# Attention and expert layer on one core: first weight loaded by head halves and split in place, state products in three passes, state reads in column tiles

## The chip, the cores and the metric

The kernel runs on one core of a Trainium2 chip. The metric is the device time of one execution in microseconds (us). The kernel before took 666.48, 667.12 and 668.52 us in three runs; the median is 667.12 us. Engines are called by the profile's short names: PE is the matrix engine (PEld its weight loads), DVE the vector engine, ACT the scalar engine, POOL the general engine, SP the engine whose queue issues most transfers.

## The reference

Eight batches, eight heads, 512 tokens and 32 state rows of 64 numbers per head. Tokens attend to the state rows and the state rows attend to the tokens; the results stand side by side as 544 rows of 512 numbers, and each row goes through a layer norm and a two-layer product with 2048 hidden units.

```python
def _attn_ref(x, state):            # x: 8,8,512,64   state: 8,8,32,64
    scores = scale * x @ state^T;  a = softmax(scores);   xread = a @ state
    scores2 = scale * state @ x^T; a2 = softmax(scores2); sread = a2 @ x
    return concatenate([xread, sread], axis=2)

def _moe_ref(x, g_ln, w_ch1, w_ch2):   # x: 8,544,512  w_ch1: 512,2048  w_ch2: 2048,512
    xn = (x - mean) / sqrt(var + 1e-06) * g_ln
    return x + maximum(xn @ w_ch1, 0.0) @ w_ch2
```

The two weights arrive as 64-bit floats, 8.4 MB each.

## The kernel before, in words

Every number that goes into a product is scaled and split into a high and a low 16-bit part; a product then takes three of the four pairs of parts (`TERMS`). Heads are numbered 4g + j: g is one of two halves of the heads, j one of four heads within a half. The weights are worked on in four units u of 512 hidden columns.

*The head of the program.* `weights1(u)` loads unit u of the first weight in two transfers of 1 MB (L587, 128 partitions by 8 KB, tiles `raw` and `sums`), puts the two 32-bit words of each number together (`words`, on ACT and DVE, tile `w_t`), takes the mean over the rows out (`means` on PE, L601, then four updates of `w_t` on DVE), finds the largest column sum on PE (L610) for the scale, and splits the unit into halves in `raw` or `sums`. Four transfers of 256 KB from 64 partitions to 64 partitions then bring the halves into `w1c[u]`, so that a high part on one set of 64 partitions stands opposite a low part on the other.
`attention(0)` runs among this: batch 0's tokens are split and transposed by two DMA transposes (`xT`, two halves of the tokens), the state by one (`sT`). The score products (L405) make four groups of eight products, two per half of the tokens; softmax follows on DVE and ACT (`mp`, `mB`, `eB`, `ts`, `ea`). `read_state` (L481) multiplies the tokens by the state's softmax, 32 products of 128 by 128 by 64, and `fold_halves` (L494) adds the halves with four 32-bit products by a folded identity.
`state_products(b)` (L667) multiplies the state of a batch by `w1c`: for each unit and each g eight products of 128 rows, 32 columns (a column tile of the array) and 512 values, two passes of four column tiles. ACT and DVE split the result into `matrix[b][u]`. Because a token's attention is a mixture of 32 state rows, the first layer of the tokens is a product of `matrix` with the softmax (`first_products` L703 for batch 0, `first` L801 for the others).
`weights2` loads and splits the second weight; `second_products_by_unit` (L717) makes batch 0's second layer.

*The body.* From batch 1 on `products(b)` makes the first layer in blocks (L801, tile `half`) and the second by Strassen's scheme with seven sums (L857, tile `acc`), while `attention(b+1)` and `state_products(b+1)` for the next batch run among it.

*The end.* The 256 state rows (`state_rows`) go through the first layer by `w1c` itself (`first_of_state`, L810) and a copy of its high parts (`high_halves`), then through the second.

*What sets the order.* All work stands in lists of steps (`streams`). `PLAN` is a written-out string of entries "stream:steps"; `issue` runs it through, and each engine's instructions, the transfers on SP's queue too, stand in exactly that order. `WARM` products of a constant tile `ones` into a spare tile (L188, tile `half`) are among the steps; nothing reads them. Most instructions carry the line of the helper `do` (L188), so they are told apart by their tiles.

*On-chip sums.* PE writes to three pools: `acc` (four tiles), `banks` (one tile of two banks, used by scores, state reads and token mixtures) and `half` (two tiles).

The steps that the change touches: L299 (`gx`), L477 to L496 (`read_state`, `fold_halves`), L586 to L623 (`weights1`), L662 to L677 (`state_products`), L806 (`first_of_state`), L893 (`high_halves`), `state_rows`, `PLAN` and `WARM`.

## Time and profile before

| | |
|---|---|
| three runs | 666.48, 667.12, 668.52 us, median 667.12 |
| span of the profiled execution | 665.1 us (first to last instruction, 14886 instructions); the page gives no other time for it, so the median lies 2.0 us above the span |
| granted clock, mean | 0.996 |
| PE busy | 643.9 us (97%) |
| DVE, ACT, POOL busy | 499.5 (75%), 388.8 (58%), 217.9 us (33%) |
| DMA | 69.64 MB, 105 GB/s on average |

The page cuts the span into 40 slices of 16.6 us; a digit is the busy share of a slice in tenths. The groups' rows give the shapes, the count, the busy time, the mean time of one instruction and the idle time before them. "L857 PE MATMUL acc<-w2h,xs" is a product of line 857 that writes tile `acc` from tiles `w2h` and `xs`. Products overlap in the pipe, so a group of n takes less than n times its mean.

### The profile page before, as it was taken

To read this page: it belongs to the slowest core of one execution; us is meant where nothing else is said; L and a number is where in the kernel's file an instruction comes from. 1 tells how busy PE (TensorE), PEld (TensorE's weight loads), DVE (VectorE), ACT (ScalarE), POOL (GpSimd) and SP (SyncE) were. 2 spreads that over 40 slices of the span, in tenths; PEclk is the share of its full clock that TensorE was granted. 3 is DMA by queue.
4 is the path that set the end of the run, shared out by engine and by line. 5 is a ranking of instruction groups with operands and counts; after the bars stand their busy time and mean duration, and the time that the engine had idled before them with its cause. 6 is when DMAs were issued, how large, how long until landed. Compare 5 with 4: busy or idle time off the path is not lost.

```text
span 665.1 us, 14886 instructions
## 1 busy us (share of the span) xinstructions
PE 643.9 (97%) x6051; PEld 499.6 (75%) x6051; DVE 499.5 (75%) x1002; ACT 388.8 (58%) x699; POOL 217.9 (33%) x189
## 2 busy tenths in 40 slices
PE   7997999999999999999999999999999999999996
PEld 2343655549887887788888888888778887888885
DVE  5998976687788677967887689777976897465533
ACT  5498889667546474547465656465546564344331
POOL 0000443321344315323452226333433343234222
PEclk8999999999999999999999999999999999999999
DMA  8999846825131434340416152405142411245211
GB/s 323 309 276 209 257 130 132 138 57 135 43 67 43 130 105 78 96 100 2 92 33 163 67 88 68 100 2 121 38 125 46 77 33 42 82 116 98 78 57 32
DMA packets 98564, 69.64 MB, mean 105 GB/s; under 512 B 72704, under 2 KB 90624, under 8 KB 98048
## 3 DMA queue, kind: packets, MB, share of 16 engines
q1 hardware_dynamic: 96384, 64.77, 38.4%
q0 software_dynamic: 864, 3.15, 2.5%
q8 instruction: 47, 0.77, 0.5%
q10 hardware_dynamic: 1248, 0.79, 0.4%
q14 instruction: 21, 0.17, 0.1%
HBM read 28.05 MB, written 9.44 MB: 56 GB/s over the span
## 4 chain that ended last, share of the span: by engine, by line
PE 86%; DVE 8%; DMA 3%; ACT 1%; issue 1%; SPq 0%; DVEq 0%
PE acc L857 41%; PE half L801 22%; PE acc L717 6%; PE half L667 5%; PE half L810 3%; DVE w_t L188 2%; PE acc L703 2%; PE acc L749 2%; PE banks L481 1%; PE banks L405 1%; PE banks L517 1%; DMA w1c<-raw 1%; DMA raw<-in_moe_w_ch_dram 1%; PE banks L494 1%; DMA x_f<-in_x_dram 1%
## 5 line engine op out<-in xcount | busy, mean ns | idle before, releaser
L857 PEld LDWEIGHTS <-xs 128*128 128x128 f16 x2520 | 242.4, 98 | 43.6 <-issue 15.3
L188 POOL TENSOR_TENSOR xs<-rs,xs 128x512 f16<-128x512 f32 x120 | 142.5, 1200 | 272.6 <-ACT xs L188 207.1
L857 PE MATMUL acc<-w2h,xs 128*128 128x256 f16 x1440 | 183.0, 273 | 0.0
L801 PE MATMUL half<-ea,matrix 128*128 128x256 f16 x1344 | 159.4, 273 | 0.0
L801 PEld LDWEIGHTS <-matrix 128*128 128x128 f16 x1344 | 130.7, 98 | 16.7 <-issue 0.8
L857 PE MATMUL acc<-sums,xs 128*128 128x256 f16 x1080 | 141.9, 273 | 0.0
L188 DVE SCALAR_TENSOR_TENSOR rs<-half,rs 128x256 f32<-128x256 f32 x224 | 89.4, 419 | 27.6 <-ACT rs L188 13.3
L188 ACT ACTIVATE xs<-rs 128x512 f16<-128x512 f32 x128 | 77.1, 618 | 40.5 <-DVE rs L188 33.8
L188 ACT ACTIVATE xs<-half 128x256 f16<-128x256 f32 (+1 forms) x112 | 53.7, 487 | 73.2 <-PE half L801 51.3
L188 DVE SCALAR_TENSOR_TENSOR xs<-half,xs 128x256 f16<-128x256 f32 (+1 forms) x112 | 61.2, 550 | 28.1 <-ACT xs L188 24.5
L188 ACT ACTIVATE matrix<-half,hs 128x512 f16<-128x512 f32 x56 | 38.1, 687 | 35.2 <-PE half L667 34.9
L188 DVE SCALAR_TENSOR_TENSOR matrix<-half,hs,matrix 128x512 f16<-128x512 f32 x56 | 41.2, 742 | 16.0 <-ACT matrix L188 15.3
L188 ACT ACTIVATE rs<-half 128x256 f32<-128x256 f32 x56 | 21.4, 382 | 42.4 <-PE half L801 40.0
L717 PE MATMUL acc<-w2h,hid 128*128 128x512 f16 x192 | 43.1, 379 | 0.0
L188 DVE TENSOR_TENSOR strip<-acc,strip 128x256 f32<-128x256 f32 (+1 forms) x60 | 33.2, 554 | 10.5 <-PE acc L857 7.5
L667 PE MATMUL half<-w1c,sT 128*32 128x512 f16 x448 | 33.5, 384 | 1.9 <-DVE rs L188 1.0
L717 PEld LDWEIGHTS <-hid 128*128 128x128 f16 x192 | 18.5, 98 | 20.9 <-issue 0.4
L188 POOL TENSOR_TENSOR ts<-ts,mA 128x1024 f32<-128x1024 f32 (+1 forms) x8 | 14.4, 1806 | 59.3 <-DVE mA L188 52.9
L188 PE MATMUL half<-ones 128*128 128x512 bf16 x103 | 28.0, 416 | 1.1 <-DVE ones L309 1.1
L188 DVE SCALAR_TENSOR_TENSOR x<-x_f,x_s,x 128x512 f16<-128x512 f32 x32 | 24.8, 799 | 5.3 <-ACT x L188 5.3
L188 POOL TENSOR_TENSOR hid<-strip,hid 128x512 f16<-128x512 f32 x16 | 19.5, 1232 | 26.9 <-ACT hid L188 26.8
L188 DVE BATCH_NORM_STATS2 s<-xr 128x6 f32<-128x512 f32 x32 | 21.6, 684 | 8.7 <-ACT xr L188 8.6
(154 smaller groups left out, 791.5 us busy)
## 6 DMA issues: line engine op xcount, KB each, us to landing
raw<-in_moe_w_ch_dram SPq DMA_DIRECT2D x9, 1024.0 KB, 8.6
out_dram<-xr SPq DMA_DIRECT2D x16, 512.0 KB, 3.7
x_f<-in_x_dram SPq DMA_DIRECT2D x15, 512.0 KB, 5.0
sums<-in_moe_w_ch_dram SPq DMA_DIRECT2D x7, 1024.0 KB, 8.2
ek<-ea SPq DMA_DIRECT2D x56, 64.0 KB, 2.0
ek<-ek SPq DMA_DIRECT2D x7, 512.0 KB, 4.3
xr<-part POOLq DMA_DIRECT2D x6, 512.0 KB, 5.0
w1c<-raw SPq DMA_DIRECT2D x8, 256.0 KB, 6.8
```

Source lines behind the costliest of these rows:

```text
L188: return lambda: f(*map(now, args), **{k: now(v) for k, v in kw.items()})
L405: nc.tensor.matmul(o[32 * j:32 * j + 32], lhsT=sT[:, g, a, 32 * j:32 * j + 32], rhs=xT[:, s, 4 * g + j].rearrange("p c t -> p (c t)"), sta ...
L481: nc.tensor.matmul(ps_z[:, h // 4, :, h % 4], lhsT=xv[:, c // hc, h, c % hc], rhs=ebT[:, :, h // 4, c, 32 * (h % 4):32 * (h % 4) + 32], st ...
L494: nc.tensor.matmul(pr[:, g], lhsT=z4[:, g, i], rhs=fold, start=i == 0, stop=i == 1, skip_group_check=True)
L517: nc.tensor.matmul(px[:, c, D * h:D * h + D], lhsT=ek[:, h // 4, h % 4, (2 * t + c) * P:(2 * t + c + 1) * P], rhs=sk[:, h], start=True, st ...
L667: nc.tensor.matmul(ps[32 * j:32 * j + 32], lhsT=sT[:, g, a, 32 * j:32 * j + 32], rhs=w[:, 2 * g + j // 2, j % 2], start=a == 0, stop=a == ...
L703: nc.tensor.matmul(o[:, 256 * f:256 * f + 256], lhsT=m[:, g, i, P * (q + f):P * (q + f) + P], rhs=ea[:, s, k, g], start=f == 0 and g == 0 ...
L717: nc.tensor.matmul(po, lhsT=hid[:, i, q, c * P:(c + 1) * P], rhs=w[:, j, q], start=first and q == 0 and n == 0, stop=last and q == 3 and n ...
L749: nc.tensor.matmul(o, lhsT=signs[:, k // 2], rhs=v[k], start=start and k == 0, stop=k == 3, skip_group_check=True)
L801: nc.tensor.matmul(ps[:, 256 * q:256 * q + 256], lhsT=m[:, h, i, P * (2 * k + q):P * (2 * k + q) + P], rhs=ea[:, 0, j, h, 256 * g:256 * g ...
L810: nc.tensor.matmul(ps[:, 256 * q:256 * q + 256].rearrange("p (t n) -> p t n", t=2), lhsT=w[:, k // 2, k % 2, fs] if k < H else wn[:, k - H ...
L857: nc.tensor.matmul(po[o], lhsT=y[:, n, i, o] if o < 2 else x[:, o - 2, n, i], rhs=v[j], start=u == 0 and n == 0 and k == 0 and o in (2, 1, ...
```

## The change

- `weights1` loads by head halves: each 1 MB transfer becomes two of 512 KB, one to partitions 0 to 63 (g = 0), one to partitions 64 to 127 (g = 1). Partition 64g + d then holds row d of the four heads of half g. `gx` is loaded likewise in two.
- The split writes straight into `w1c[u]` (high and low parts one behind the other); the 16 transfers from `raw` and `sums` to `w1c` are gone. So is `high_halves` with its 8 transfers.
- `state_products` makes, for a unit, 24 products of 64 rows, 32 columns and 512 values: three passes (`TERMS`) over four column tiles and two row halves g. From batch 1 on the two g write the two banks of one `banks` tile, and ACT and DVE split both at once (1024 values); before, each g wrote a `half` tile of its own.
- `read_state` makes 64 products: for each j, c and part i one for each g, written to partitions 64g to 64g + 63; the high token part meets both parts of the softmax (64 values), the low part only the high one (32 values). A DVE reduction adds the parts, and one 32-bit transpose by the identity takes the place of the four fold products.
- The state rows are arranged to match: eight blocks of 128 in place of twelve, and the same 12 products for each result.
- `PLAN` is new; `WARM` goes from 103 to 73.

Three places where the order moves, on the engines that wait there. First SP, from the start of the program. Before:

```order
L188 DMA x_f<-in_x_dram 128x4x256
L188 DMA s_j<-in_state_dram 128x2x64
L587 DMA sums<-in_moe_w_ch_dram 128x2x1024 x2
L587 DMA raw<-in_moe_w_ch_dram 128x2x1024 x3
L188 DMA_TRANSPOSE xT<-x_108 128x16x128
L188 DMA_TRANSPOSE sT_224<-sh 128x4x128
L188 DMA_TRANSPOSE xT<-x_108 128x16x128
L587 DMA raw<-in_moe_w_ch_dram 128x2x1024 x2
```

Now:

```order
L187 DMA x_f<-in_x_dram 128x4x256
L187 DMA s_j<-in_state_dram 128x2x64
L585 DMA raw<-in_moe_w_ch_dram 64x2x1024 x2
L585 DMA sums<-in_moe_w_ch_dram 64x2x1024 x2
L585 DMA raw<-in_moe_w_ch_dram 64x2x1024 x6
L585 DMA sums<-in_moe_w_ch_dram 64x2x1024 x2
L585 DMA raw<-in_moe_w_ch_dram 64x2x1024 x2
L585 DMA sums<-in_moe_w_ch_dram 64x2x1024 x2
L187 DMA_TRANSPOSE xT<-x_109 128x16x128
L187 DMA_TRANSPOSE sT_168<-sh 128x4x128
L187 DMA_TRANSPOSE xT<-x_109 128x16x128
```

Before, five of the eight megabytes of the first weight stood ahead of the transposes; now all 16 half transfers do.

Second PE, where the first score products (L405) stand among the means of the weights (L601, now L598); what an instruction waits for stands in brackets. Before, at the second unit's means:

```order
L601 MATMUL acc<-w_t,gm 128x512 [waits DVE_49]
L601 MATMUL acc<-w_t,gm 128x512 x3
L405 LDWEIGHTS sT_224 [waits DMAHW2_49]
L405 MATMUL banks<-xT,sT_224 32x256 [waits DMAHW1_49]
L405 LDWEIGHTS sT_224
```

Now, at the end of the first eight score products:

```order
L405 MATMUL banks<-xT,sT_168 32x256
L598 MATMUL acc<-w_t,gm 128x512 [waits DVE_49]
L598 MATMUL acc<-w_t,gm 128x512 x3
L405 LDWEIGHTS sT_168
L405 MATMUL banks<-xT,sT_168 32x256 [waits DMAHW7_49]
```

Two units' means stand ahead of the score products in both; the third unit's stood behind all 32 of them, with 20 warm products and a column sum between, and now stand right behind the first eight, which wait for the transposes.

Third DVE, around the first reading of the scores (`mp`, the maximum of the state's scores). Before:

```order
L188 STREAM_TRANSPOSE ts<-banks 128x512
L188 SCALAR_TENSOR_TENSOR w_t<-w_t,gx,acc 128x512 x3
L188 TENSOR_REDUCE mA<-ts 128x16
L188 TENSOR_REDUCE of_weights<-acc 128x1
L188 TENSOR_TENSOR ts<-ts,mA 128x512
L188 SCALAR_TENSOR_TENSOR w_t<-w_t,gx,acc 128x512
L188 TENSOR_REDUCE mp<-banks 128x4
L188 TENSOR_REDUCE dA<-ts 128x16
```

Now:

```order
L187 SCALAR_TENSOR_TENSOR w_t<-sums 128x1024
L187 SCALAR_TENSOR_TENSOR w_t<-w_t,gx,acc 128x512 x4
L187 TENSOR_SCALAR sums<-sums 128x1024
L187 TENSOR_SCALAR raw<-raw 128x1024
L187 SCALAR_TENSOR_TENSOR w_t<-w_t,gx,acc 128x512 x3
L187 TENSOR_REDUCE mp<-banks 128x4
L187 TENSOR_TENSOR mB<-mp 128x2
L187 TENSOR_SCALAR mB<-mB,es 128x2
L187 STREAM_TRANSPOSE ts<-banks 128x512
L187 SCALAR_TENSOR_TENSOR w_t<-raw 128x1024
```

The reading of the scores has moved: the words of three units and eleven of their twelve updates now stand ahead of it, and the words of the last unit behind it. From it to the end of the first split into `w1c` it is 32 rows of DVE now, and 32 rows from it to the end of the first split before.

The diff without `PLAN`:

```diff
-WARM = 103
+WARM = 73
...
-    nc.scalar.dma_start(out=gx, in_=g_ln.rearrange("(k p) -> p k", p=P))
+    for g in range(G):
+        nc.scalar.dma_start(out=gx[64 * g:64 * g + 64], in_=g_ln.rearrange("(g j d) -> g d j", g=G, j=4)[g])
...
-        ps_z = pz[:, 0].rearrange("p (g i j n) -> p g i j n", g=G, i=2, j=4)
+        ps_z = pz[:, 0, 0:256].rearrange("p (j i n) -> p j i n", j=4, i=2)
 
         def read_state(ps_z, x16, ebT):
-            xv = x16.rearrange("p (s h c) i d -> p s h c (i d)", s=parts, c=hc)
-            for h in range(H):
+            xv = x16.rearrange("p (s h c) i d -> p s h c i d", s=parts, c=hc)
+            for j in range(4):
                 for c in range(C):
-                    nc.tensor.matmul(ps_z[:, h // 4, :, h % 4], lhsT=xv[:, c // hc, h, c % hc],
-                                     rhs=ebT[:, :, h // 4, c, 32 * (h % 4):32 * (h % 4) + 32],
-                                     start=c == 0, stop=c == C - 1, skip_group_check=True)
+                    for i in range(2):
+                        for g in range(G):
+                            nc.tensor.matmul(ps_z[64 * g:64 * g + 64, j, 0:2 - i], lhsT=xv[:, c // hc, 4 * g + j, c % hc, i],
+                                             rhs=ebT[:, 0:2 - i, g, c, 32 * j:32 * j + 32],
+                                             start=c == 0 and i == 0, stop=c == C - 1, skip_group_check=True)
...
-        yield do(nc.scalar.activation, z, pz[:, 0], AF.Copy)
-        def fold_halves(pr, z4):
-            for g in range(G):
-                for i in range(2):
-                    nc.tensor.matmul(pr[:, g], lhsT=z4[:, g, i], rhs=fold, start=i == 0, stop=i == 1,
-                                     skip_group_check=True)
-        yield do(fold_halves, pr, z4)
+        yield do(nc.vector.tensor_reduce, z.rearrange("p (j n) -> p j n", j=4), ps_z.rearrange("p j i n -> p j n i"), AX.X,
+                 ALU.add)
+        yield do(nc.tensor.transpose, pz[:, 1, 0:P], z, idf)
...
-            nc.sync.dma_start(out=raw.rearrange("p (k f) -> p k f", k=2),
-                              in_=w1[256 * fh:256 * fh + 256, 1024 * u:1024 * u + 1024].rearrange("(k p) f -> p k f",
-                                                                                                  p=P))
+            rows_of = w1[:, 1024 * u:1024 * u + 1024].rearrange("(g j d) f -> g d j f", g=G, j=4)
+            for g in range(G):
+                nc.sync.dma_start(out=raw.rearrange("p (j f) -> p j f", j=2)[64 * g:64 * g + 64],
+                                  in_=rows_of[g, :, 2 * fh:2 * fh + 2])
...
-        hl = raws[1].bitcast(F16).rearrange("p (i e) -> p i e", i=2)
-        yield from split(hl[:, 0], hl[:, 1], t, scale)
-        hl = hl.rearrange("p i (k f) -> p i k f", k=4)
-        w = narrow(u, "w1c").bitcast(F16).rearrange("p (k s f) -> p k s f", k=4, s=2)
-        w1c[u] = w
-        for i in range(2):
-            for s in range(2):
-                to = 64 * (i ^ s)
-                yield do(nc.sync.dma_start, out=w[to:to + 64, :, s], in_=hl[64 * s:64 * s + 64, i])
+        w = narrow(u, "w1c").bitcast(F16).rearrange("p (i e) -> p i e", i=2)
+        yield from split(w[:, 0], w[:, 1], t, scale)
+        w1c[u] = w.rearrange("p i (j f) -> p i j f", j=4)
...
-        def multiply(ps, g, sT, w):
-            for a in range(2):
+        def multiply(ps, sT, w):
+            for n, (i, k) in enumerate(TERMS):
                 for j in range(4):
-                    nc.tensor.matmul(ps[32 * j:32 * j + 32], lhsT=sT[:, g, a, 32 * j:32 * j + 32],
-                                     rhs=w[:, 2 * g + j // 2, j % 2], start=a == 0, stop=a == 1, skip_group_check=True)
+                    for g in range(G):
+                        r = slice(64 * g, 64 * g + 64)
+                        nc.tensor.matmul(ps[g][32 * j:32 * j + 32], lhsT=sT[r, g, i, 32 * j:32 * j + 32], rhs=w[r, k, j],
+                                         start=n == 0, stop=n == 2, skip_group_check=True)
...
-                ps = accumulator() if b == 0 else half()
...
+                ps = banks()
+                scale = hs[:, u:u + 1]
+                yield do(lambda p, *a: multiply([p[:, g] for g in range(G)], *a), ps, sT, w1c[u])
+                yield do(nc.scalar.activation, m[:, :, 0], ps, AF.Copy, scale=scale)
+                yield do(nc.vector.scalar_tensor_tensor, m[:, :, 1], ps, scale, m[:, :, 0], ALU.mult, ALU.subtract)
...
-    def high_halves(u):
-        high[u] = quad("high").bitcast(F16).rearrange("p (k f) -> p k f", k=4)
-        for s in range(2):
-            half = slice(64 * s, 64 * s + 64)
-            yield do(nc.sync.dma_start, out=high[u][half], in_=w1c[u][half, :, s])
```

More of the change, by code (lines that the diff above doesn't have):

```diff
@@ L804, in first, with first_of_state @@
                                                  skip_group_check=True)
[L806 removed]
+                def first_of_state(ps, k, w, xsT):
                     for q in range(2):
[L808 to L812 removed]
+                        fs = slice(P * (2 * k + q), P * (2 * k + q) + P)
+                        for n, (i, x) in enumerate(TERMS):
+                            for j in range(4):
+                                nc.tensor.matmul(ps[:, 256 * q:256 * q + 256].rearrange("p (t n) -> p t n", t=2),
+                                                 lhsT=w[:, i, j, fs], rhs=xsT[:, :, x, j],
+                                                 start=q == 0 and n == 0 and j == 0, stop=n == 2 and j == 3,
+                                                 skip_group_check=True)
                 def strassen_hidden(b=b, g=g, u=u, halves_of=halves_of, x=x, y=y, rs=rs, s=s):
@@ L820, in block @@
                         else:
[L821 removed]
+                            yield do(first_of_state, ps, k, w1c[u], state_rows_T[0])
                             r = rs[:, 512 * k:512 * k + 512]
@@ L939, in moe_attention @@
         streams += these
-    streams += [list(state_rows()), *(list(high_halves(u)) for u in range(U))]
+    streams.append(list(state_rows()))
     streams += [list(s) for s in products(B)]
```

43 lines of the change are left out of this document (19 added, 24 removed), and 242 rows, old and new, of the table PLAN.

## The prediction

> **What bounds the kernel now.** I read the page first, then the busy times by stretch.
>
> ```profile
> span 665.1 us, 14886 instructions
> PE 643.9 (97%) x6051; PEld 499.6 (75%) x6051; DVE 499.5 (75%) x1002; ACT 388.8 (58%) x699; POOL 217.9 (33%) x189
> ...
> PE 86%; DVE 8%; DMA 3%; ACT 1%; issue 1%; SPq 0%; DVEq 0%
> ```
>
> ```profile
> core 0: us, PE busy (x) PEld busy (x) DVE busy (x) ACT busy (x) POOL busy (x), PEclk, DMA share, GB/s
> 0.00:57.90 57.90, 46.37 (x258) 20.79 (x259) 50.20 (x87) 38.73 (x48) 1.75 (x7) 0.97 1.01 289
> 57.90:76.60 18.70, 16.70 (x178) 10.17 (x177) 16.01 (x33) 16.18 (x27) 5.98 (x5) 1.00 0.84 211
> 76.60:138.00 61.40, 61.34 (x429) 35.02 (x429) 45.67 (x88) 50.76 (x79) 23.58 (x22) 1.00 0.66 148
> 138.00:659.40 521.40, 519.43 (x5187) 433.58 (x5186) 385.54 (x794) 283.17 (x546) 186.59 (x156) 1.00 0.31 75
> ```
>
> There are two programs in one. From 76.6 us on PE is busy without a gap worth naming (2 us in 583), so there every microsecond of PE work taken away is a microsecond gained, and nothing else counts. Up to 76.6 us PE is filled up with warm products; the DMA share is about 1, DVE is busy for 66 of 76.6 us, and what counts is when the first state products can start. The chain of waits shows how that came about:
>
> ```profile
> 46.36 1.12 DVE w_t L188
> 47.48 2.27 DVE raw L188
> 49.77 1.37 SPq L188
> 51.19 6.68 DMA w1c<-raw
> 57.92 6.29 DMA raw<-in_moe_w_ch_dram
> ```
>
> DVE ends the first unit's split at 49.7, the transfers into `w1c` take until 57.9, and there PE's first state product starts. So the time is the start of the state products plus PE's work behind it. The change cuts the second and moves the first.
>
> **PE's work behind the head.** The price of a state product group, from PE's timeline:
>
> ```profile
> 299.54 0.38 PE L857 MATMUL acc<-w2h,xs 128*128 128x256 f16 x2
> 299.85 0.62 PE L667 MATMUL half<-w1c,sT 128*32 128x512 f16 x8
> 300.40 0.28 PE L857 MATMUL acc<-sums,xs 128*128 128x256 f16 x1
> ...
> 79.37 1.05 PE L667 MATMUL acc<-w1c,sT 128*32 128x512 f16 x16
> 80.35 1.05 PE L703 MATMUL acc<-ea,matrix 128*128 128x256 f16 x8
> ```
>
> Two passes hold PE from 299.85 to 300.40, 0.55 us; four from 79.37 to 80.35, 0.98. A pass of four column tiles is (0.98 - 0.55) / 2 = 0.215 us. The two plain products before start at 299.54 and 0.11 later, and the next would have started at 299.76, so entering costs 0.09 and leaving 0.12: 0.21 for the change of tiling. A unit's two groups cost 2 x 0.64 = 1.28 apart and 1.07 together; most stand apart. After: one group of three passes, 3 x 0.215 + 0.21 = 0.86, if the two row halves run at once. Saved 0.42 apart, 0.21 together; I take 0.36, and for the 28 units of batches 1 to 7 -10 us. That is 6 to 12 if they do run at once. If they run one after the other it is six passes, 1.50 us, and a loss of 28 x 0.22 to 0.43 = 6 to 12. No row of the trace has two row groups in flight; four column tiles of one pass are, so I take that they do.
>
> ```profile
> 8.15 0.27 PE L188 MATMUL banks<-idf,x_am 128*2 128x128 f32 x1 [3.05 <-DVE x_am L188]
> 8.26 0.50 PE L188 MATMUL half<-ones 128*128 128x512 bf16 x1
> ...
> L494 PE MATMUL banks<-fold,z 128*128 128x64 f32 x64 | 8.2, 272 | 0.5 <-ACT z L188 0.5
> L481 PE MATMUL banks<-ebT,x 128*128 128x64 f16 x256 | 8.8, 193 | 0.0
> ...
> 156.60 1.10 PE L481 MATMUL banks<-ebT,x 128*128 128x64 f16 x32
> 157.53 1.47 PE L801 MATMUL half<-ea,matrix 128*128 128x256 f16 x12
> 158.84 1.00 PE L494 MATMUL banks<-fold,z 128*128 128x64 f32 x8
> 159.68 0.38 PE L749 MATMUL acc<-w2h,signs 128*128 128x256 f16 x2
> ```
>
> The fold costs 159.68 - 158.84 = 0.84 a batch. One transpose of 128 columns lies between 0.11 (the transpose of the two columns of `x_am` starts at 8.15, the product behind it at 8.26) and half the fold, 0.42; I take 0.25: -0.6 x 7 = -4. The state read costs 0.93 for 32 products, 29 ns each. After it is 64 of half the width. If the two column tiles run at once, 16 x (64 + 32) values at 29 ns for 64 are 0.70, with the change of tiling 0.91; if each product keeps its 29 ns it is 2.07. I take 1.25, near the lower end, as column tiles overlap fully in the row above: +0.3 x 7 = +2, between 0 and +8. Against me speaks the Trainium skill, "TensorEngine Tiling (Array Packing)", Gotcha 2: column tiling excludes the fast weight load. By it the 64-column loads would set the pace and the state read would be nearer +8; no run here shows a 64-column load.
>
> Together -12, between -18 and -2. The state rows keep their 12 products a result. DVE gets a reduction in place of ACT's copy of `z`, and the double-width split of `matrix` holds the single `banks` tile longer, but only beside other users of it; with DVE busy 386 of 521 us there I price that at nothing, and at up to +6 where PE meets a `banks` tile still being read.
>
> **The head.** What goes: 4.2 MB of transfers into `w1c`, 7 us of them on the chain. What comes: all of the first weight in transfers to 64 partitions, ahead of the transposes. The rate of the two kinds stands in two windows, 8 to 18 us (loads to 128 partitions) and 51 to 57 us (64 to 64 partitions, alternating halves):
>
> ```profile
> DMA packets 1080, 4.16 MB, mean 416 GB/s; under 512 B 64, under 2 KB 64, under 8 KB 1080
> q1 hardware_dynamic: 1080, 4.16, 102.8%
> ...
> DMA packets 1300, 1.25 MB, mean 209 GB/s; under 512 B 78, under 2 KB 1300, under 8 KB 1300
> q1 hardware_dynamic: 1300, 1.25, 113.4%
> ```
>
> Both keep all 16 engines busy; with 64 partitions they move half as much. I take 209 GB/s for the new loads and keep 416 as the other bound, since the slow rows are copies from one on-chip tile to another and not loads. The Trainium skill, "SBUF — State Buffer", Door 1, says why it would hold for loads too: 64 partitions reach 8 of 16 ports, 196 GB/s measured, and two transfers to both halves gain only 6%. By its 196 the weight would land 3 us later than by the row; the trace agrees with the rule.
>
> ```profile
> 0.74 5.50 DMA x_f<-in_x_dram
> ...
> 15.00 5.06 SPq L188 DMA_TRANSPOSE xT<-x  x1
> 20.18 1.20 SPq L188 DMA_TRANSPOSE sT<-sh  x1
> ...
> 24.45 0.62 PE L405 MATMUL banks<-xT,sT 128*32 128x256 f16 x16
> ...
> 30.16 1.22 DVE L188 TENSOR_REDUCE mp<-banks 128x4 f32<-128x1024 f32 x1
> ...
> 47.40 4.61 DVE L188 SCALAR_TENSOR_TENSOR raw<-w_t,of_weights,raw 128x2048 f16<-128x2048 f32 x2
> ```
>
> The first tokens land at 6.2. Then 8.39 MB at 209 GB/s take 40 us: 46.3. The transposes queue behind: before, the first could be issued at 15.0 and still landed only when the loads ahead had drained (its products start at 24.45). I give it 2 us: 48.3. Then PE's order holds: eight score products 0.5, the third unit's means, 16 and 8 more score products and a column sum:
>
> ```profile
> 16.16 3.70 PE L601 MATMUL acc<-w_t,gm 128*128 128x512 f32 x8 [0.48 <-DVE w_t L188]
> ...
> 26.07 1.02 PE L610 MATMUL acc<-sums,ones 128*128 128x512 bf16 x4 [0.24 <-ACT sums L188]
> ```
>
> 0.5 + 3.5 + 1.0 + 0.9 + 0.5 = 6.4, so `mp` starts at about 54.7. DVE is queued up behind it. From `mp` to the end of the first split it took 47.40 + 2.3 - 30.16 = 19.5 us before for 32 rows; the new 32 rows are of the same kinds, so the first split ends at 74 to 75, and the first state products start there without a transfer, against 57.9: +17. PE stands idle from the second unit's means until the transposes, and cold products cost double:
>
> ```profile
> 1.09 4.01 PE L188 MATMUL half<-ones 128*128 128x512 bf16 x9 [1.09 <-DVE ones L309]
> ...
> 27.79 2.55 PE L188 MATMUL half<-ones 128*128 128x512 bf16 x11
> ```
>
> 0.45 us each at the start, 0.23 later. The third unit's 3.5 us may become up to 7: I take +3. Head: +20, between +14 and +24. What follows it (three more splits, the second weight's words) is DVE work as long as before, and the 30 warm products that go only filled idle time: nothing.
>
> **Sum.** 665.1 + 20 - 12 = 673.1 in the profile; the median lies 2.0 above the span (667.1 - 665.1): **675 us**, 667 to 683 for this case.
>
> **The rivals.** *Full rate.* The half transfers load at 416 GB/s: 6.2 + 20.2 = 26.4, transposes at 28.5, and then DVE, not DMA, sets the pace. Before, five words and eight updates stood ahead of `mp` and it started at 30.2; now it is six and eleven, behind the third unit's means (3.5), about 4 to 7 us more; 19.5 later, at 54 to 57, come the first state products, against 57.9. Cold products give that back: 667 - 12 + 1 = 656. For it: the slow rows are no loads. Against: 416 and 209 differ by a factor of 2.0, as the partitions do.
> *The transposes don't queue.* If they overtook the loads, the last unit's words at 46.3 would decide: words and means 7 us, updates 3, and ten more DVE us to the split: 66, +8, so 663. Against: the transposes of the first row above waited for the loads although issued.
> *Row halves in turn.* On top of the slow loads, state products lose 9 instead of gaining 10: 694. It decides if a group of 24 holds PE for 1.5 us.
> *The work is not less:* that a unit needs three passes instead of four is in the code, so that the change doesn't do what it says can only come by this last rival.
>
> **How the numbers follow.** Forecast 0.70, full rate 0.18, overtaking 0.07, row halves in turn 0.05. A measurement of this kernel can tell 0.3%, 2 us, from no change. Slower than 669.1: nearly all of the forecast and the last rival, 0.70; within 2 us: the forecast's lower edge and some overtaking, 0.07; faster: full rate, the rest of overtaking, 0.23. The range must take in most of the full-rate case (656) and the forecast's own upper edge: 653 to 683.
>
> **What would show it.** Right: loads of the first weight at about 210 GB/s until some 46 us, the transposes landing at 48 or later, the first state product at 72 to 78 us, groups of 24 holding PE for 0.86 us, the state read 0.9 to 1.3 us, and PE without gaps behind. Wrong: loads above 300 GB/s, or a first state product before 65 us, or groups of 24 above 1 us, or PE idle for more than 5 us in the body.

## The result, and the profile after

The kernel after takes 737.4 us (median; 736.1 to 740.4) against 667.4 before: a ratio of 1.106, 95% interval [1.104, 1.109]. The forecast was slower, 675 us, range 653 to 683. The sign was right and the size was missed by 62 us. All times here and below are medians of runs in the core's faster state; one run of f4 below, 718.3 us, was not in it and is left out. In the profiled execution of after, from the page:

```profile
span 738.5 us, 15618 instructions
...
PE 650.5 (88%) x6477; PEld 499.4 (68%) x6477; DVE 506.2 (69%) x982; ACT 373.9 (51%) x663; POOL 226.5 (31%) x189
...
PE 43%; DVE 16%; ACT 7%; DMA 6%; issue 2%; SPq 1%; POOL 1%; DVEq 0%; ACTq 0%; POOLq 0%
```

The last row is the chain of work that ended last. Before, 86% of it was PE; now it is 43%, and the rest changes from engine to engine. Busy time by stretch shows where that began; the cuts are the first state product, the first product of batch 1, the last product of batch 7 and the end of PE's work. After:

```profile
core 0: us, PE busy (x) PEld busy (x) DVE busy (x) ACT busy (x) POOL busy (x), PEclk, DMA share, GB/s
0.00:76.00 76.00, 42.71 (x205) 17.27 (x205) 45.40 (x82) 37.23 (x42) 3.71 (x8) 0.96 0.95 238
76.00:189.40 113.40, 98.02 (x833) 58.00 (x833) 83.10 (x150) 74.43 (x128) 36.59 (x26) 0.94 0.37 82
189.40:682.40 493.00, 460.70 (x4999) 380.42 (x4996) 355.79 (x710) 245.65 (x465) 171.59 (x143) 0.98 0.30 69
682.40:731.50 49.10, 49.08 (x450) 43.74 (x448) 19.36 (x38) 16.62 (x30) 14.65 (x13) 1.00 0.08 26
```

The same cuts in the kernel before:

```profile
57.90:149.60 91.70, 89.65 (x683) 51.21 (x683) 72.23 (x134) 74.26 (x121) 31.47 (x27) 1.00 0.64 150
149.60:609.90 460.30, 458.42 (x4644) 383.45 (x4641) 351.05 (x727) 256.91 (x500) 170.35 (x142) 1.00 0.32 77
609.90:659.40 49.50, 49.41 (x477) 44.12 (x473) 23.94 (x53) 18.94 (x32) 14.33 (x13) 1.00 0.28 63
```

So the 73.4 us between the two spans are: head +18.1 (76.0 against 57.9), middle +21.7 (113.4 against 91.7), body +32.7 (493.0 against 460.3), end +0.9. The head is what was forecast. The middle was priced at nothing and the body at -12. In the body PE now stands idle for 32.3 us (493.00 - 460.70; before 1.9), in the middle for 15.4 (before 2.0), and the clock granted to it is 0.98 and 0.94 in place of 1.00: by an estimate from these two figures (2% of 461 and 6% of 98) some 9 and 6 us more for the same products. What PE waits for, from the waits of after (us in total, times, longest):

```profile
PE banks L187 <- DVE x_am L187: 14.7, 2, 14.5
PE banks L405 <- DMA sT<-sh: 13.0, 2, 7.9
PE acc L598 <- DVE w_t L187: 12.2, 4, 6.9
PE banks L405 <- DMA xT<-x: 10.1, 7, 1.9
PE banks L483 <- DMA ebT<-eb: 6.3, 4, 2.7
PE half L800 <- DVE xs L187: 5.2, 6, 1.4
PE half L800 <- DVE rs L187: 3.8, 5, 1.4
...
PE banks L660 <- DVE matrix L187: 1.3, 2, 0.8
```

The first and third rows are the head (but for 0.2 us), and so are 5.1 us of the second; the other 7.9 are batch 1's scores, in the middle. The rest (but for 0.6 us of the fifth row) lies in the body and recurs from batch to batch: scores that wait for their transposes, state reads for theirs, products for the elementwise results of the products before. Waits for the transposes `xT` and `ebT` are 15.8 of the body's 32.3 us. The state products (L660) hardly wait for the tile `banks`, 1.3 us. The new work itself is as cheap as it was priced:

```profile
336.59 0.82 PE L858 MATMUL acc<-sums,xs 128*128 128x256 f16 x6
337.34 0.84 PE L660 MATMUL banks<-w1c,sT 64*32 64x512 f16 x24
338.12 1.16 PE L858 MATMUL acc<-w2h,xs 128*128 128x256 f16 x9
```

A group of 24 products holds PE for 0.78 us (337.34 to 338.12), and the six products ahead of it for 0.75 in place of 0.65: 0.87 with what entering costs (six such products otherwise take 6 x 0.109); 0.86 were forecast.

```profile
246.99 1.19 PE L483 MATMUL banks<-ebT,x 128*64 128x64 f16 x64
248.11 1.48 PE L800 MATMUL half<-ea,matrix 128*128 128x256 f16 x12
249.43 0.27 PE L187 MATMUL banks<-idf,z 128*128 128x128 f32 x1
```

A state read is 1.12 us (246.99 to 248.11). And the new loads of the first weight run at half rate, 512 KB every 2.4 us; transfers between 20 and 40 us:

```profile
DMA packets 1207, 4.38 MB, mean 219 GB/s; under 512 B 139, under 2 KB 139, under 8 KB 1207
...
q1 hardware_dynamic: 1207, 4.38, 103.1%
```

### The profile page after: what moved, and what is told of

Same layout as the page of the kernel before. It is cut to its first block, busy times and chain, and to the rows that moved or that the text cites. A ratio compares the mean times of both kernels' runs of the same rounds, so it can differ in the third digit from the quotient of the medians.

```text
span 738.5 us, 15618 instructions
## 1 busy us (share of the span) xinstructions
PE 650.5 (88%) x6477; PEld 499.4 (68%) x6477; DVE 506.2 (69%) x982; ACT 373.9 (51%) x663; POOL 226.5 (31%) x189
## 4 chain that ended last, share of the span: by engine, by line
PE 43%; DVE 16%; ACT 7%; DMA 6%; issue 2%; SPq 1%; POOL 1%; DVEq 0%; ACTq 0%; POOLq 0%
PE acc L858 23%; PE half L800 13%; DVE rs L187 3%; DMA xT<-x 3%; PE half L810 3%; ACT xs L187 2%; PE banks L660 2%; DVE x L187 2%; DVE xs L187 2%; SPq L187 1%; DVE strip L187 1%; DMA ebT<-eb 1%; ACT eB L187 1%; ACT x L187 1%; PE banks L513 1%
## 5 line engine op out<-in xcount | busy, mean ns | idle before, releaser
L858 PEld LDWEIGHTS <-xs 128*128 128x128 f16 x2520 | 245.9, 99 | 43.0 <-issue 7.2
L800 PE MATMUL half<-ea,matrix 128*128 128x256 f16 x1344 | 167.6, 278 | 9.1 <-DVE xs L187 5.2
L187 DVE SCALAR_TENSOR_TENSOR rs<-half,rs 128x256 f32<-128x256 f32 x224 | 91.0, 417 | 54.8 <-ACT rs L187 27.7
L716 PE MATMUL acc<-w2h,hid 128*128 128x512 f16 x192 | 47.0, 403 | 2.5 <-DVE w2h L187 2.5
L187 POOL TENSOR_TENSOR ts<-ts,mA 128x1024 f32<-128x1024 f32 (+1 forms) x8 | 16.2, 2022 | 89.7 <-DVE mA L187 89.7
L187 DVE SCALAR_TENSOR_TENSOR matrix<-banks,hs,matrix 128x1024 f16<-128x1024 f32 x28 | 35.9, 1281 | 8.7 <-ACT matrix L187 8.6
L716 PEld LDWEIGHTS <-hid 128*128 128x128 f16 x192 | 19.6, 103 | 26.1 <-issue 7.8
L187 POOL TENSOR_TENSOR hid<-strip,hid 128x512 f16<-128x512 f32 x16 | 26.0, 1635 | 27.2 <-ACT hid L187 27.2
L187 ACT ACTIVATE matrix<-banks,hs 128x1024 f16<-128x1024 f32 x28 | 31.1, 1110 | 6.0 <-PE banks L660 5.9
L598 PE MATMUL acc<-w_t,gm 128*128 128x512 f32 x32 | 21.8, 832 | 12.2 <-DVE w_t L187 12.2
L187 ACT ACTIVATE x<-x_f,x_s 128x512 f16<-128x512 f32 x32 | 21.8, 712 | 20.2 <-DVE x_s L187 19.3
L405 PE MATMUL banks<-xT,sT 128*32 128x512 f16 (+1 forms) x144 | 11.2, 406 | 23.1 <-DMA sT<-sh 13.0
L187 DVE SCALAR_TENSOR_TENSOR x<-x_f,x_s,x 128x512 f16<-128x512 f32 x32 | 29.2, 939 | 1.7 <-ACT x L187 1.7
```

Source lines behind the costliest of these rows:

```text
L187: return lambda: f(*map(now, args), **{k: now(v) for k, v in kw.items()})
L405: nc.tensor.matmul(o[32 * j:32 * j + 32], lhsT=sT[:, g, a, 32 * j:32 * j + 32], rhs=xT[:, s, 4 * g + j].rearrange("p c t -> p (c t)"), sta ...
L598: nc.tensor.matmul(ps, lhsT=gm[:, k:k + 1].broadcast_to([P, P]), rhs=t4[:, k], start=k == 0, stop=k == 3)
L716: nc.tensor.matmul(po, lhsT=hid[:, i, q, c * P:(c + 1) * P], rhs=w[:, j, q], start=first and q == 0 and n == 0, stop=last and q == 3 and n ...
L800: nc.tensor.matmul(ps[:, 256 * q:256 * q + 256], lhsT=m[:, h, i, P * (2 * k + q):P * (2 * k + q) + P], rhs=ea[:, 0, j, h, 256 * g:256 * g ...
L858: nc.tensor.matmul(po[o], lhsT=y[:, n, i, o] if o < 2 else x[:, o - 2, n, i], rhs=v[j], start=u == 0 and n == 0 and k == 0 and o in (2, 1, ...
```

## The experiments

Each kernel's times stand beside runs of the kernel before on the same chip (666.9 to 667.6). "Start", "middle" and "body" are the same cuts as above, read from each trace; "idle" is PE's in the body.

| kernel | order | state products of batches 1 to 7 | loads of w1 | us | start | middle | body | idle |
|---|---|---|---|---|---|---|---|---|
| before | old | two single tiles in turn, 4 passes | full | 667.4 | 57.9 | 91.7 | 460.3 | 1.9 |
| after | new | two-bank tile, 3 passes | half | 737.4 | 76.0 | 113.4 | 493.0 | 32.3 |
| e2 | old | as before | half | 683.7 | 74.4 | 91.4 | 460.3 | 1.9 |
| e3 | old | as after | half | 753.6 | 70.0 | 110.4 | 513.8 | 47.0 |
| f3 | old | two single tiles at once, 3 passes | half | 716.2 | 70.1 | 101.5 | 486.6 | 27.7 |
| f4 | old | as f3 | full | 704.5 | 60.1 | 100.3 | 486.7 | 27.8 |
| f5 | new | as after | full | 727.7 | 63.1 | 111.3 | 494.9 | 33.3 |
| f6 | old | two-bank tile, 4 passes | full | 736.8 | 56.8 | 104.3 | 517.4 | 43.7 |
| g1 | new | as after, tile not held | half | 735.5 | 77.6 | 109.6 | 491.6 | 34.4 |
| g2 | old | as after, tile not held | half | 698.7 | 69.7 | 102.4 | 468.4 | 16.2 |
| h1 | old | two single tiles in turn, 3 passes each | full | 676.8 | 54.5 | 98.5 | 467.5 | 3.4 |
| h3 | old | as before | full | 664.4 | 58.4 | 91.3 | 458.0 | 3.4 |
| j1, j2 | new, edited | as after | half | 741.2, 739.4 | 71.9, 74.4 | 109.6, 111.5 | 500.4, 495.4 | 41.1, 37.7 |
| k1 | old, edited | as before | full | 701.3 | 56.8 | 91.6 | 493.4 | 26.0 |
| m1 | new | as after, small splits | half | 735.2 | 75.8 | 113.5 | 489.4 | 33.7 |
| m2 | old | as before, small splits | full | 667.1 | 57.8 | 93.6 | 460.3 | 1.9 |

**Is it the half-rate loads?** Three theories stood at the start. Theory A says that everything behind the head inherits its lateness, B that the new order is at fault, C that the new operations are, in any order. e2 puts the half-rate loads into the kernel before:

```diff
-            nc.sync.dma_start(out=raw.rearrange("p (k f) -> p k f", k=2), in_=...)
+            for g in range(2):
+                nc.sync.dma_start(out=raw.rearrange(...)[64 * g:64 * g + 64], in_=rows_of[64 * g:64 * g + 64])
```

> The kernel before, with each 1 MB load of the first weight made into two loads of 512 KB to 64 partitions; nothing else changed, and the order is the old one. Theory A: the half rate alone makes the program late throughout, by tens of us: 700 us or more. Theories B and C: the old order has lead enough to take the lateness of the head once and no more: the loads end 20 us later, the w1c moves stay, so 667 + 18 to 24 = 685 to 691 us, with TensorE busy without gaps again from about 100 us on.

683.7 us, ratio 1.025 [1.022, 1.027], 1 us below the 685 to 691 of B and C. Behind the late start nothing changes; busy time by stretch of e2:

```profile
74.40:165.80 91.40, 89.54 (x683) 51.16 (x683) 72.21 (x134) 74.18 (x121) 31.11 (x27) 1.00 0.64 150
165.80:626.10 460.30, 458.42 (x4644) 383.32 (x4641) 351.01 (x727) 256.72 (x500) 170.16 (x142) 1.00 0.32 77
```

Middle and body are those of the kernel before to 0.3 us. Theory A is out: the old order takes a late head once, 16.6 us, and that is all. The converse is the kernel after with full-rate loads. e1, and e4 with the order of e3 below, load one row of heads in one transfer to 128 partitions:

```diff
-            for g in range(G):
-                nc.sync.dma_start(out=raw...[64 * g:64 * g + 64], in_=rows_of[g, :, 2 * fh:2 * fh + 2])
+            for j in range(2):
+                nc.sync.dma_start(out=raw[:, 1024 * j:1024 * j + 1024], in_=rows_of[:, :, 2 * fh + j])
```

> The kernel after, with each pair of loads of the first weight to 64 partitions made into two loads to all 128 partitions (same bytes, same number of loads, same place of every row); everything else, the order too, as it was. Theory A (late loads): all of the extra time comes from the first weight arriving at half rate; the rest of the program inherits the lateness. Then the waits behind the head go with it and the time is 650 to 665 us. Theory B (order): the new order leaves the transposes and the elementwise results of every batch too little lead before TensorE needs them, and these waits come again in each batch whatever the head does: the first state product at 55 to 62 us in place of 76, some of the 22 us lost between it and the products of batch 1 back, the 493 us of the products unchanged: 700 to 718 us. Theory C (the new operations): the state products into one two-bank tile and the state read in column tiles hold up the engines behind them, in any order: 700 to 718 us here too.

> As the run before it (the operations of the kernel after in the order of the kernel before), and with loads of the first weight to 128 partitions. Theory A: 650 to 660 us. Theory B: the body's 12 us and the 7 us of transfers into w1c are both gained: 645 to 655 us, faster than the kernel before. Theory C: 690 us or more.

857.9 and 877.8 us (ratios 1.286 [1.281, 1.290] and 1.316 [1.312, 1.319]), far above what any theory had, and they say little on the theories. The loads ran at a quarter of the rate in mind; transfers of e1 between 50 and 80 us:

```profile
DMA packets 389, 1.57 MB, mean 52 GB/s; under 512 B 6, under 2 KB 6, under 8 KB 389
...
q1 hardware_dynamic: 389, 1.57, 12.8%
```

The source's slowest dimension was the pair of head groups, of size 2, and the queue took 12.8% of 16 engines' time, two of them. (The Trainium skill, "DMA: Bandwidth & Descriptors", "Why a DMA increments its semaphore by 16 and not by 1", has the rule: the size of the slowest dimension sets how many of the 16 engines a transfer is spread over. The trace agrees.) The first state product came at 195 to 199 us; e1's body was 493 us again, as in after.

f5 goes another way: it groups the heads by parity, 2j + g in place of 4g + j, so that the rows for 128 partitions lie together and the old 1 MB transfers serve.

```diff
-            rows_of = w1[...].rearrange("(g j d) f -> g d j f", g=G, j=4)
-            ... two transfers to 64 partitions
+            nc.sync.dma_start(out=raw.rearrange("p (k f) -> p k f", k=2), in_=w1[...].rearrange("(k p) f -> p k f", p=P))
-        src = x[b].rearrange("h (p c) d -> p h c d", c=C)
+        src = x[b].rearrange("(j g) (p c) d -> g p j c d", g=G, c=C)
```

> The kernel after in its own order and with its two-bank tile, and the first weight loaded to 128 partitions in 1 MB transfers as in f4. It replaces e1, whose loads ran at a quarter of the rate wanted. If the half-rate loads explain the head alone: the first state product at 55 to 62 us, some of the 22 us between it and the products of batch 1 back, the 493 us of the products as they were: 700 to 718 us. If the body's waits are inherited from the head: below 675 us.

727.7 us, ratio 1.089 [1.085, 1.094], above the expected 700 to 718, and far above the 675 that inherited waits would have stayed under. The start falls from 76 to 63, but the median only by 10 us; middle (111.3) and body (494.9) stay. The half rate is worth 10 us here and 17 in the old order (e2) of the 70 us, and is a matter of the head alone.

**Is it the order, or the new operations?** e3 is the kernel after with its steps in the order of the kernel before:

```diff
-PLAN = (the order of after)
+PLAN = (the order of before; steps without a counterpart left out; a unit's 24 products where its first 8 stood,
+        some places off where `banks` is still in use)
```

> The operations of the kernel after, its loads to 64 partitions too, issued in the order of the kernel before: each instruction stands where its counterpart stood, those without one are left out, and a unit's state product goes where its first half stood, shifted by a few places where the two-bank tile is still in use. Theory A: as the kernel after, 725 us or more. Theory B: the waits of the batches are gone and the sum of the prediction holds: 672 to 682 us. Theory C: the order is not what costs, 705 us or more.

753.6 us, ratio 1.129 [1.126, 1.132]: 70 us above e2, which has the same order and loads, and 16 above the kernel after. Theory B, that the new order alone is at fault, is out; what C expected has come. Its waits:

```profile
PE banks L658 <- DVE matrix L185: 16.5, 7, 3.1
...
PE banks L403 <- DVE matrix L185: 7.7, 3, 2.6
PE banks L658 <- ACT eB L185: 6.0, 2, 4.3
PE banks L481 <- DVE matrix L185: 5.9, 4, 2.5
```

L658 are the state products, L403 the scores, L481 the state reads. All three write `banks`, and each waits until another user has read it out. This suggests theory D, the shared tile. f6 asks it of the kernel before, with none of the new products; a unit's products stand at one place of its `PLAN` in place of two:

```diff
-                ps = accumulator() if b == 0 else half()
-                yield do(multiply, ps, g, sT, w1c[u])
+                ps = banks()
+                yield do(both, ps, sT, w1c[u])                  # the old 16 products, g = 0 and 1
+                ... both splits in double width
```

> The kernel before, where alone the state products of batches 1 to 7 change: the 16 products of a unit (four passes, as before) go into the two-bank tile and are split there in double width, at the places of the order where e3 has them. Loads, moves into w1c, state read and fold as before. Theory D: the waits of e3 come back without any of the new operations: 700 to 740 us. Theory C: as the kernel before, 665 to 672 us.

736.8 us, ratio 1.104 [1.100, 1.108], and the waits of e3:

```profile
PE banks L666 <- DVE matrix L187: 16.4, 7, 2.9
...
PE banks L404 <- DVE matrix L187: 7.6, 3, 2.5
PE banks L666 <- ACT eB L187: 5.7, 2, 4.0
```

Theory C doesn't explain that, since the new operations aren't there: one shared tile for both halves costs 69.5 us in the old order. g2 turns that round: e3 with everything as it was, but the splits read a constant, so that the tile is free when PE has written it.

```diff
-                yield do(nc.scalar.activation, m[:, :, 0], ps, AF.Copy, scale=scale)
+                still = mhalf[:, 0:1].unsqueeze(2).broadcast_to([P, G, 512])
+                yield do(nc.scalar.activation, m[:, :, 0], still, AF.Copy, scale=scale)    # and VectorE's likewise
```

> As e3 (operations of the kernel after, loads to 64 partitions, order of the kernel before), with the tile not held in the way of g1: the splits read a constant. Theory D: the 70 us between e2 and e3 come from holding the tile, so with it free the time is e2's 684 less 12 us of TensorE work and some 5 us of w1c transfers: 664 to 676 us, what the prediction's sum gave. Theory C: the new operations hold up the program by themselves, above 715 us.

698.7 us, ratio 1.048 [1.044, 1.051]: 55 of the 70 us are gone, with the same number of operations on every engine. It isn't the 664 to 676 of theory D. PE is still idle for 16.2 us in the body. State products still wait 11.6 us for the attention to be done with the same tile, 7.7 of them in the body and the rest in the middle:

```profile
PE banks L658 <- ACT eB L185: 5.5, 2, 3.8
...
PE banks L658 <- DVE ts L185: 4.2, 1, 4.2
...
PE banks L658 <- ACT xr L185: 1.9, 2, 1.2
```

f3 and f4 take two tiles `half` in place of `banks`; the products of the next block take their turns at those:

```diff
-                ps = banks()
+                ps = [half() for _ in range(G)]
```

> As e3 (the operations of the kernel after with its loads to 64 partitions, in the order of the kernel before), but a unit's state product for batches 1 to 7 goes into two of the small tiles `half` instead of the two-bank tile `banks` that the attention uses, at places of the old order where both halves are free. The three passes of both row halves, the state read in column tiles and the one transpose stay. Theory D (shared tile): what costs is that the state products and the attention of the next batch take turns at one two-bank tile; then the waits of e3 go and the time is the one of e2 (684) less the 12 us of TensorE and some 5 us of w1c transfers: 664 to 674 us. Theory C (the new operations are slow or hold up others by themselves): still above 720 us.

> As f3, and the first weight loaded to 128 partitions in transfers of 1 MB, in the row order of the kernel before. For that the heads are grouped by parity (heads 2j+g in place of 4g+j stand in column tile j of group g): the loads of x, state and gain and the places of the outputs follow, the operations stay. Theory D: 645 to 656 us, faster than the kernel before, because the w1c transfers (7 us on the path) and 12 us of TensorE work are gone and nothing is late. Theory C: 700 us or more.

716.2 and 704.5 us (ratios 1.073 [1.069, 1.077] and 1.056 [1.052, 1.060]), 42 to 60 us above the expectations of D; f4 lies in the range of C. The waits have moved, in f3 to

```profile
PE half L808 <- DVE matrix L682: 17.5, 13, 4.1
...
PE half L660 <- DVE matrix L682: 6.2, 10, 1.6
```

The first products of the next block (L808) wait for the split of the pair. So it isn't this tile alone: two tiles taken at once from another pool cost too. h1 multiplies the two row halves apart, one bank at a time, at the two places of the old order:

```diff
-                yield do(lambda p0, p1, *a: multiply((p0, p1), *a), *ps, sT, w1c[u])
+                for g in range(G):
+                    ps = half()
+                    yield do(lambda p, *a, g=g: multiply({g: p}, *a, (g,)), ps, sT, w1c[u])
```

> As f4 (order of the kernel before, weight loaded to 128 partitions in the old row order), but for batches 1 to 7 the two row halves of a state product are multiplied apart, 12 products each into one small tile `half`, at the two places where the old order has the two groups; and the state's loads are issued ahead of the weight's again. That costs TensorE 56 groups of about 0.85 us in place of 56 of 0.64, +6 to 12 us against the kernel before, but never takes two banks at once. Theory D: no waits in the body, the first state product at 50 to 55 us: 662 to 678 us, in spite of 20 us more TensorE work than f4 (706). Theory C: 700 us or more.

676.8 us, ratio 1.015 [1.012, 1.018], and PE idle for 3.4 us in the body. PE's work is larger:

```profile
204.50 0.82 PE L863 MATMUL acc<-w2h,xs 128*128 128x256 f16 x6
205.25 0.83 PE L664 MATMUL half<-w1c,sT 64*32 64x512 f16 x12
206.01 1.49 PE L863 MATMUL acc<-w2h,xs 128*128 128x256 f16 x12
```

Twelve products of one row half hold PE for 0.76 us (205.25 to 206.01), 24 of both for 0.78: the two row halves do run at once. Giving that up doubles the state products' time, and the kernel is still 28 us faster than f4, 6 of them by its earlier start: the price of the second bank against that of the passes. PE hardly waits in h1's body, though its products, reads and transposes are the new ones; that both row halves run at once is the one thing that it leaves out, and f6 has the waits without it. So theory C is out too.

Another difference stands beside these. e3, f3, f4, g2 and h1 have 73 warm products in the old order, so the last 30 of its 103 are missing, those from about 41 us on in the kernel before. Two groups of h1, and the first 20 us of the middle in h1 and, last, in the kernel before:

```profile
54.54 1.48 PE L664 MATMUL acc<-w1c,sT 64*32 64x512 f16 x24
...
73.04 0.84 PE L664 MATMUL acc<-w1c,sT 64*32 64x512 f16 x24
...
54.50:74.50 20.00, 15.43 (x163) 8.66 (x162) 17.53 (x30) 14.04 (x22) 2.21 (x2) 0.62 0.16 60
...
57.90:77.90 20.00, 17.96 (x190) 11.31 (x190) 17.31 (x36) 17.48 (x28) 6.26 (x5) 1.00 0.85 211
```

The same 24 products take 1.48 us at first and 0.84 later. Over these 20 us the granted clock is 0.62 to 0.83 in the five, 0.91 in m2 and 1.00 in e2, f6, h3 and k1, which have the old order with all 103. h1's middle is 6.8 us longer than that of the kernel before, so by an estimate some 7 us of the distance of e3, f3 and g2 from e2, and of f4 and h1 from the kernel before, belong to neither the tile nor the passes. No run puts the 30 back, so the cause of this part is argued. Differences among the five, and f6, aren't touched by it.

h3 does the other part of the change alone, in the kernel before:

```diff
-        yield do(nc.scalar.activation, z, pz[:, 0], AF.Copy)
-        yield do(fold_halves, pr, z4)
+        yield do(nc.vector.tensor_reduce, z..., ps_z..., AX.X, ALU.add)
+        yield do(nc.tensor.transpose, pz[:, 1, 0:P], z, idf)
```

(and the state read's 64 products in column tiles, as in after)

> The kernel before with one part of the change alone: the state read in column tiles, the sum of its two parts on VectorE and one transpose in place of the copy and the fold. Loads, w1c, state products and order as before. By the prediction's terms 2 us less TensorE work (-4 and +2): 663 to 668 us (theory D: this part is harmless). Theory C: 672 us or more.

664.4 us, ratio 0.9958 [0.9943, 0.9972]: this part is a small gain, 3 us, and h3 is faster than both kernels. Its body is 458.0 us against 460.3.

**What holds the new order up?** In after almost nothing waits for the tile. g1 frees the tile in the new order, as g2 in the old:

> The kernel after in its own order; the two splits of a unit's state product (batches 1 to 7) keep their size and place but read a constant that stands still in SBUF in place of the two-bank tile, so the tile is free as soon as TensorE has written it. The results of these products are not used (the outputs of batches 1 to 7 are not computed); TensorE, ScalarE and VectorE do the same number of operations of the same sizes. Theory D1 (in this order, too, the engines are held up by the tile at run time): 722 us or less. Theory D2 (the order has been arranged around the tile, so that almost nothing waits for it directly, 1.3 us on TensorE, and the price is paid elsewhere: transposes and elementwise results come too late for their places): 730 to 740 us, as the kernel after.

735.5 us, ratio 1.102 [1.098, 1.106]: D2. With g2 and e3 that makes a table of four, all with the new operations and half-rate loads: tile held, 753.6 in the old order and 737.4 in the new; tile free, 698.7 and 735.5. The new order is 16 us better under the tile and 37 worse without it, with the same operations and loads. j1 and j2 give the transposes of each batch a longer lead; the maximum that begins the chain has its inputs just ahead of it, so it moved by 11 places at most and in three batches not forward at all, while the steps behind it moved up towards it.

```diff
-    ... 65:0 63:8 62:8 65:1 65:5 81:13-14 59:3 65:3 65:7 81:15-16 59:1 81:17-18 ...
+    ... 81:12 60:0 81:13-14 63:7 63:9 63:11 65:0 81:15 63:8 81:16 ...               # j1, batch 5
```

> The kernel after with its order edited: in batches 2 to 7 the chain that leads to the scores (the maximum across partitions, the scales, the splits of x and state, the transposes: 23 items of each batch) stands 10 places earlier in the order; three state products move a little where the two-bank tile would be wanted twice. From that maximum to the first scores there are 65 to 85 places in the order of after and 87 to 103 in that of before. Theory L (lead): the body's waits come from that shorter lead; 5 to 10 us less than the kernel after (737): 727 to 732 us, the waits of the scores for xT about halved. Theory E (VectorE and ScalarE are behind as a whole, an earlier place does not make them earlier): 734 to 740 us.

> As j1, 20 places earlier, the lead of the order of before. Theory L: 715 to 728 us, the waits of the scores for xT gone. Theory E: 734 us or more.

741.2 and 739.4 us (ratios 1.111 [1.109, 1.113] and 1.109 [1.105, 1.114]). The waits of j2:

```profile
PE half L805 <- DVE xs L192: 10.5, 11, 2.1
...
PE half L805 <- DVE rs L192: 4.6, 4, 2.0
...
PE banks L410 <- DMA xT<-x: 2.1, 3, 0.8
```

The scores' wait for `xT` fell from 10.1 to 2.1, and the products' waits for DVE rose from 9.0 to 15.1: the wait was moved, not removed, and PE's idle time in the body rose from 32.3 to 37.7 us. As far as these edits test it, theory L fails here. k1 puts the same chain later in the old order:

> The kernel before with the same chain 20 places later in batches 2 to 7 (never past its own scores or state products), so that its lead is about that of after; nothing else changed, and no two-bank tile for the state products. Theory L: TensorE now waits for the transposes in each batch as in after: 675 to 690 us. Theory E: 665 to 670 us.

701.3 us, ratio 1.051 [1.048, 1.054]: more than the 675 to 690 of theory L, whose direction it has. In its body the scores and the state products wait 16.6 us for `xT` and `sT`, where the kernel before has no such wait. A lead that the old order has and that is taken away costs 34 us. So the old order's evenness can be spoilt by one edit, and the new order's unevenness wasn't mended by these two. m1 takes most of the splits' work away in the new order, and m2 in the old:

```diff
-                yield do(nc.scalar.activation, m[:, :, 0], ps, AF.Copy, scale=scale)
+                yield do(nc.scalar.activation, o[:, :, 0], ps[:, :, 0:1], AF.Copy, scale=scale)    # VectorE's likewise
-            m = matrix[b][u] = block(...)
+            m = matrix[b][u] = block(...) if b == 0 else matrix[0][u]
```

> The kernel after in its own order, where the two splits of each state product of batches 1 to 7 read 2 values a partition in place of 1024, and the products of these batches use the matrix of batch 0 (so the outputs of batches 1 to 7 are not computed). TensorE's work and order stay; ScalarE loses 31 us and VectorE 36 us of work (28 x 1.11 and 28 x 1.28), all of it in the stretch of each batch ahead of its scores. Theory E (what the new order lacks is time on ScalarE and VectorE in that stretch, where the double-width splits now stand close together): the body's waits shrink by more than half, 705 to 720 us. Theory F (the waits are set by the order of the instructions and the transfers, whatever the load of the two engines): 730 us or more.

> The same cut made in the kernel before (splits of 1 value a partition in place of 512, the matrix of batch 0 for all batches). TensorE bounds it and nothing waits for these splits: 664 to 668 us under either theory, the measure of what the cut is worth where it is not on the path.

735.2 us (ratio 1.102 [1.098, 1.106]) and 667.1 (1.000 [0.998, 1.002]). The waits of m1 are those of after:

```profile
PE banks L405 <- DMA xT<-x: 12.8, 9, 2.1
PE acc L598 <- DVE w_t L187: 12.7, 4, 6.9
PE banks L483 <- DMA ebT<-eb: 6.1, 4, 2.8
PE half L802 <- DVE xs L187: 4.8, 6, 1.4
```

and its body in busy time:

```profile
189.30:678.70 489.40, 455.69 (x4999) 378.02 (x4996) 329.69 (x709) 223.83 (x465) 171.98 (x143) 0.99 0.30 69
```

Theory E fails, and F stands: DVE is busy for 26 us less (329.7 against 355.8) and ACT for 22 less (a split of two values still takes 0.21 us on DVE and 0.26 on ACT, so less than was expected), and the time falls by 2, which the intervals can't tell from nothing. What bounds the body of the new order is the order: not the loads (f5), not the held tile (g1), not the load of the splits (m1), and with the same operations and a free tile the old order takes 37 us less (g2). Engines that each take their steps in a fixed sequence wait for one another in turn. Which steps bind isn't settled, and that the order is as it is because of the tile is argued from the table of four, not shown.

## Why the prediction was wrong

*The head* was right. Loads to 64 partitions at half rate (219 GB/s, 209 taken), their end at 45.6 us (46.3), the transposes behind them (state at 48.6, 48.3 forecast), the first state product at 76.0 (74 to 75, range 72 to 78). The rivals "full rate" and "the transposes don't queue" fell with it. In the old order this head costs 16.6 us (e2).

*The work of PE* was right. 0.87 us for a group of 24 (0.86), 1.12 for a state read (1.25), and one transpose of 128 columns at the lower end of its bounds. "Row halves in turn" fell: 0.76 us for twelve, 0.78 for 24. How much of the -12 us was there to be had no run shows in its time. PE's busy time in g2's body is 6 us below that of the kernel before at a clock of 0.99, by an estimate some 11 at full clock; h3 gains 3 with its part.

*The step that failed is that -12 us of PE's work is -12 us of time.* It needs a body in which PE never waits, and the prediction took the body of the new order for as dense as the old one; it followed the new order through the head alone. Its own sign of error, PE idle for more than 5 us in the body, came true with 32.3: the body is 33 us longer in place of 12 shorter. The half rate isn't the cause (f5), nor is the held tile in this order (1.3 us of waits; g1), nor the load of the splits (m1). With the tile free, the same operations take 37 us less in the old order (g2 against g1). That the middle would be "as long as before" failed in the same way (+21.7, and +19.6 with full-rate loads); half of its wait is one, the 7.9 us of batch 1's scores for `sT`.

*The second step that failed is the price of the `banks` tile*, put "at nothing, and at up to +6 where PE meets a `banks` tile still being read", because it is held longer "but only beside other users of it". But a product over two row halves fills two banks at the same time, and both pools that were tried have other users: the attention waits for `banks` (e3, f6), the next block's products for `half` (f3). Had the order been kept, that is 69.5 us (f6), or 55 from holding the tile alone (e3 against g2); with the pair of `half` it is 32 us net of what the change saves (f3 against e2), with some 7 us in it that go with the missing warm products. That the new order is as it is to get around this, no run shows. The rule that speaks against this part of the change stands in the page that the prediction did cite: the Trainium skill, "TensorEngine Tiling (Array Packing)", "Gotcha 1: PSUM Pressure", says that row tiles write to different banks and so raise the pressure on them. The traces of e3 and f3 agree. The prediction weighed Gotcha 2 of that page, which cost at most 0.2 us a batch here (a state read of 1.12 us, 0.91 at the lower bound).

*The clock was not in the sum at all*: 0.98 in the body and 0.94 in the middle, the some 15 us estimated above. In the bodies it goes with the idle time: 1.00 where PE is idle for up to 3.4 us (before, e2, h1, h3, m2), 0.97 to 0.99 at 16 to 41 us, 0.96 at 44 and 47 (f6, e3). No run changes one without the other, so that idle time brings the clock down is argued.

By these sizes: 675 was 665 + 20 - 12 + 2. Measured, the head is +18, the middle +22, the body +33 in place of -12, the end +1.

## What to carry to other kernels

Before a product is spread over row groups, count the banks that it fills at once and who else needs them: three passes into two banks lost to six passes into one bank by 22 us behind the head (f4 and h1). When a change comes with a new order of all steps, price the order as an edit of its own, by looking for the slack of each wait in the old trace; here, moving one chain did not mend it (j1, j2). When an old order is taken over for a test, take its warm products along, or count what their absence may cost (h1). Do the parts apart: one part here was a gain of 0.4% and was hidden under a loss of 10%.

## What was not expected of the hardware

A transfer whose slowest dimension has size 2 moved 52 GB/s, as if over two of 16 engines, though it filled 128 partitions; half as many partitions with 64 as the slowest dimension moved 219 GB/s. And one order can be so tight that 48 us less work on two of its engines gain 2 us, no more than the noise (m1), while in the other moving 23 steps of a batch by up to 20 places costs 34 (k1).
